# One queue instead of two for the opening loads of a sparse matmul

## The chip, the cores and the metric

The kernel runs on one core of one Trainium2 chip. The metric is the device time of one execution in microseconds; a time that is given for a kernel is the median of its runs. Beside the runs there is one profiled execution, from which every row of a view comes.

## The reference

Two of every four weights along the contraction axis are kept, those of largest magnitude, and the pruned matrix multiplies x; a bias is added.

```python
B, S, D = 16, 512, 1024            # x: (B, S, D), w: (D, D), b: (D), all bf16
wg = w.reshape(D // 4, 4, D)
mag = jnp.abs(wg)
order = jnp.argsort(mag, 1)
thr = jnp.take_along_axis(mag, order[:, 2:3, :], 1)     # the second largest of four
wp = (wg * (mag >= thr)).reshape(D, D)
return jnp.einsum("bsd,df->bsf", x, wp) + b
```

## The kernel before

x is taken as 8192 rows, in 64 tiles of 128 rows. TensorE (PE) does all products: for each tile, 8 slices of the contraction axis by 2 halves of 512 output columns, accumulated in PSUM. DVE adds the bias on the way out of PSUM and ACT's queue stores the tile.

The weights have to be pruned first. They are worked on in six pieces (`pieces`): four of 256 columns for the upper half of the contraction axis (group 0), then two of 512 columns for the lower half (group 1). For a piece, DVE takes magnitudes (`abs`), maxima and minima of pairs (`hi`, `lo`), the threshold (`t1`, `t2`, `thr`), a mask and the product of weight and mask (`mult`), which it writes to `wp`. For pieces 2 and 3 ACT takes the magnitudes. In `wp` the four members of a group of four lie beside each other in a partition, so x must be in the same order to be multiplied by it: that is done for x tiles 0 to 6, which are loaded in rows (`load_x`) and transposed on PE (`T3a` is the transpose of tile 3, four matmuls against an identity), copied out of PSUM by ACT (`C3a`), and multiplied by each piece as it becomes ready (`M3.0yp` is tile 3 with part of piece 0). The partial sums are staged in SBUF (`S`, `U`). Later tiles use `wp_nat`, the pruned weights in the natural order, to which SP's queue copies `wp` by DMA (`W0.0` and the like), and x that a transposing DMA on SP's queue has loaded (`xlead`, `xlow`, `xb`).

The order of instructions on PE, DVE, ACT and SP in the opening is written out by hand as four lists of such names, and `seq` ties each instruction to the one before it on its engine. Ahead of these lists stand the opening's loads, on SP's queue and on ACT's, and the fillers: PE multiplies a constant, first six times over 512 columns, then fourteen times over 128, before the first transpose. DVE's list begins with `abs0a abs0b hi0a lo0 hi0b`: the magnitudes of piece 0 in two halves. PE's begins with `T3a T4a T5a T6a T2a M3.0yp`, so tiles 3 and 4, then 5 and 6, then 2 are wanted in that order.

`LATE` is the number of last tiles whose result is stored in two halves, each as soon as it is ready, rather than in one.

The lines that the prediction names: L138 is the filler, L193 the transpose, L198 its copy by ACT, L169 and L159 DVE's pruning steps, L229 the products with `wp`, L242 those with `wp_nat`, L98 the call that issues a load, a spread or a store, L112 the transposing loads of `xlead`.

Of the kernel before, what the change touches and what calls it, by code (L numbers as in the profile page):

```python
# [11 lines left out]
def kernel(  # L12
# [30 lines left out]
    STG = 8  # L43
    SOLO = 6
    GROUPS = ((0, 3), (3, 6), (6, 7))
    LATE = 6
    sizes = (4, 8, 8, 8, 8, 8, 8)
    batches = []
    t0 = NPK + LEAD
# [23 lines left out]
    def pe(i):  # L73
        return seq("pe", i)
# [4 lines left out]
    def act(i):  # L79
        return seq("act", i)  # L80
# [15 lines left out]
    def issue(eng, out_, in_):  # L96
        q = nc.sync if eng == "sp" else nc.scalar
        return seq(eng, q.dma_start(out_, in_))  # L98

    def load_w(g, c0, c1, ma=0, mb=4, eng="sp"):  # L100
        issue(eng, w_sb[:, g, ma:mb, c0:c1], wv[:, g, ma:mb, c0:c1])

    def load_x(ta, tb, eng="sp"):
        xs = const.tile([P, tb - ta, HK], bf16, name=f"x_{ta}")
        issue(eng, xs[:], xf[ta * P:tb * P, :HK].rearrange("(t p) k -> p t k", p=P))
        for t in range(ta, tb):
            x_sb[t] = xs[:, t - ta, :]
# [7 lines left out]

    xnat, held = {}, {}

    load_w(0, 0, 256, 0, 2)
    load_w(0, 0, 256, 2, 4, "act")
    load_x(5, 7, "act")  # L120
    act(nc.scalar.activation(spark[:], nc.const_aps.tensor(1.0, [P, 1], bf16), Act.Abs))
    load_x(3, 5)
    load_x(2, 3)
    load_w(0, 256, 512)
    load_x(0, 2)
# [10 lines left out]
    def filler(n, rep=1):  # L136
        for _ in range(n):
            pe(nc.tensor.matmul(warm_ps[:, :rep * P], lhsT=nc.const_aps.tensor(1.0, [P, P], bf16),  # L138
                                rhs=nc.const_aps.tensor(1.0, [P, rep * P], bf16), start=True, stop=True))
# [251 lines left out]
    def run(queues):  # L391
        while any(queues.values()):
            moved = False
            for eng, toks in queues.items():
                while toks and all(n in written for n in needs(eng, toks[0])):
                    emit(eng, toks[0])
                    tok = toks.pop(0)
                    written.add(tok)
                    if tok[0] == "M" or tok[0].islower():
                        written.update(atoms(tok))  # L400
                    moved = True
            assert moved, queues

    filler(6, 4)
    filler(14)
    run({eng: order[eng].split() for eng in order})

    def load_nat(ta, tb):
# [26 lines left out]
    def evac(o, ps, c0, c1, add=None):  # L435
        if add is None:
            dve(nc.vector.tensor_tensor(o[:, c0:c1], ps, bias_sb[:, c0:c1], op=Alu.add))  # L437
        else:
            dve(nc.vector.tensor_tensor(o[:, c0:c1].rearrange("p (n c) -> p n c", n=2),  # L439
                                        ps.rearrange("p (n c) -> p n c", n=2), add, op=Alu.add))  # L440
# [4 lines left out]
    def store(eng, t, o, c0=0, c1=Dout):  # L445
        issue(eng, rows(t)[:, c0:c1], o[:, c0:c1])
# [25 lines left out]
    for bi, (tb, nb) in enumerate(batches):  # L472
        if bi:
            load_batch(bi + 1)
        for j in range(nb):
# [9 lines left out]
            else:  # L485
# [4 lines left out]
                for h in range(2):  # L490
                    evac(o, pss[h][:], h * FH, (h + 1) * FH)
                    if t >= NT - LATE:
                        store("act", t, o, h * FH, (h + 1) * FH)
                if t < NT - LATE:
                    store("act", t, o)
# [30 lines left out]
```

## Time and profile before

| what | us |
|---|---|
| median of 3 runs | 232.76 (232.62 to 232.9) |
| profiled execution | 232.89 |
| its span, first to last instruction | 231.1 |
| PE busy in the span | 226.6 |
| DVE busy | 107.9 |
| ACT busy | 14.0 |

The span is shorter than the execution's time by what lies around the first and last instruction. "Busy" for PE counts overlapping matmuls once, with modelled ends; the start-to-start distance of matmuls tells their pace. In a row of a timeline the first number is the start in us from the span's start, the second the duration of the group, then the engine (a q behind it is its queue or sequencer), the line, the operation, what is written and read, and how many instructions the row holds; in square brackets stands the idle time before it and what ended it. PEld is the load of a matmul's stationary operand. In a row of DMA issues the last number is the time from issue to landing.

### The profile page before, as it was taken

The page shows a single profiled execution, that of the slowest core. Times are in us where ns is not written, and L with a number is a line of the kernel's source. Part 1 is how long each engine was busy: PE and PEld are TensorE (multiplying, and loading weights), DVE is VectorE, ACT ScalarE, POOL GpSimd, SP SyncE. Part 2 cuts the span into 40 slices and gives each one's busy share as a digit, 9 for nine tenths or more (in the row PEclk, how much of TensorE's full clock was granted, in tenths as well). Part 3 has the DMA queues.
Part 4 walks back from the last instruction along what each step waited for, and adds up shares of the span by engine and source line. Part 5 has one row for each costly group of instructions (what it writes and reads, how often), then busy time and mean ns, then how long its engine had stood idle before and what let it go on. Part 6 is the DMA issues. An engine that isn't in the chain of part 4 may idle for free.

```text
span 231.1 us, 2851 instructions
## 1 busy us (share of the span) xinstructions
PE 226.6 (98%) x1142; PEld 110.9 (48%) x1162; DVE 107.9 (47%) x200; ACT 14.0 (6%) x27; POOL 17.6 (8%) x15
## 2 busy tenths in 40 slices
PE   8999999999999999999999999999999999999995
PEld 5986444444444444444444444444444444444443
DVE  3999877844424424424424424423423423433434
ACT  2874100000000000000000000000000000000000
POOL 1000199700000000000000000000000000000000
PEclk9999999999999999999999999999999999999999
DMA  6999999997399422991259821693128932122122
GB/s 203 276 197 280 164 217 223 297 320 252 124 206 232 155 91 72 237 281 64 75 116 252 222 94 71 162 298 134 65 91 198 273 122 83 54 91 91 53 86 91
DMA packets 79308, 38.19 MB, mean 165 GB/s; under 512 B 64192, under 2 KB 71744, under 8 KB 79296
## 3 DMA queue, kind: packets, MB, share of 16 engines
q1 hardware_dynamic: 68384, 20.75, 43.6%
q10 hardware_dynamic: 10912, 17.27, 20.9%
q8 instruction: 9, 0.15, 0.3%
q14 instruction: 3, 0.02, 0.0%
HBM read 3.28 MB, written 16.78 MB: 87 GB/s over the span
## 4 chain that ended last, share of the span: by engine, by line
PE 98%; issue 0%; DVE 0%
PE ps L242 88%; PE ps L229 5%; PE tp L242 2%; PE ps L138 2%; PE tp L193 1%; PE ps L193 0%; DVE o L437 0%
## 5 line engine op out<-in xcount | busy, mean ns | idle before, releaser
L242 PE MATMUL ps<-wp_nat,xb 128*128 128x512 bf16 (+1 forms) x831 | 178.9, 375 | 0.9
L242 PEld LDWEIGHTS <-xb 128*128 128x128 bf16 x848 | 82.2, 98 | 97.7
L437 DVE TENSOR_TENSOR o<-ps,bias_sb 128x512 bf16<-128x512 f32 (+1 forms) x112 | 71.6, 677 | 113.7 <-PE ps L242 111.4
L433 POOL TENSOR_TENSOR st<-st,bias_sb 128x1024 f32<-128x1024 f32 x8 | 16.7, 2142 | 0.0
L242 PE MATMUL ps<-wp_nat,xlead 128*128 128x512 bf16 x63 | 14.7, 379 | 0.1
L242 PEld LDWEIGHTS <-xlead 128*128 128x128 bf16 x88 | 8.6, 98 | 10.2
L229 PE MATMUL ps<-wp,xt 128*128 128x256 bf16 (+1 forms) x130 | 12.8, 258 | 0.0
L439 DVE TENSOR_TENSOR o<-ps,st 128x512 bf16<-128x512 f32 x16 | 11.1, 691 | 2.8 <-PE ps L242 2.2
L229 PEld LDWEIGHTS <-xt 128*128 128x128 bf16 x130 | 10.9, 98 | 1.1
L242 PE MATMUL ps<-wp_nat,xlow 128*128 128x512 bf16 x47 | 10.6, 379 | 0.1
L264 ACT COPY st<-ps 128x512 f32<-128x512 f32 x14 | 7.4, 600 | 3.2 <-PE ps L229 3.1
L242 PEld LDWEIGHTS <-xlow 128*128 128x128 bf16 x48 | 4.7, 98 | 5.7
L159 DVE TENSOR_TENSOR mag<-mag,hi 128x256 bf16<-128x256 bf16 (+2 forms) x15 | 6.1, 435 | 0.1
L159 DVE TENSOR_TENSOR wp<-w_sb,mag 128x256 bf16<-128x256 bf16 (+2 forms) x15 | 6.1, 435 | 0.1
L242 PE MATMUL tp<-wp_nat,xlead 128*128 128x512 bf16 x23 | 5.8, 380 | 0.0
L138 PE MATMUL ps<-const-bfloat16-1.0 128*128 128x128 bf16 (+1 forms) x20 | 4.2, 408 | 0.8 <-PEq L510 0.8
L169 DVE TENSOR_SCALAR mag<-w_sb 128x512 uint16<-128x512 uint16 (+2 forms) x5 | 2.3, 473 | 3.5 <-DMA w_sb<-in_w_dram 3.5
L138 PEld LDWEIGHTS <-const-bfloat16-1.0 128*128 128x128 bf16 x20 | 2.3, 146 | 2.4 <-issue 2.4
L159 DVE TENSOR_TENSOR hi<-mag 128x512 bf16<-128x512 bf16 (+2 forms) x7 | 3.2, 458 | 0.1
L159 DVE TENSOR_TENSOR lo<-mag 128x512 bf16<-128x512 bf16 (+1 forms) x6 | 3.1, 509 | 0.0
L193 PEld LDWEIGHTS <-x 128*128 128x128 bf16 x28 | 2.3, 124 | 0.3 <-DMA x<-in_x_dram 0.2
L422 POOL COPY pruned<-wp 128x1 bf16<-128x1 bf16 x1 | 0.2, 187 | 26.7 <-DVE wp L159 26.7
(18 smaller groups left out, 18.8 us busy)
## 6 DMA issues: line engine op xcount, KB each, us to landing
out_dram<-o ACTq DMA_DIRECT2D x58, 256.0 KB, 2.4
wp_nat<-wp SPq DMA_DIRECT2D x14, 128.0 KB, 3.2
out_dram<-o ACTq DMA_DIRECT2D x10, 128.0 KB, 1.7
w_sb<-in_w_dram SPq DMA_DIRECT2D x2, 512.0 KB, 5.5
w_sb<-in_w_dram SPq DMA_DIRECT2D x3, 256.0 KB, 5.1
x<-in_x_dram SPq DMA_DIRECT2D x2, 256.0 KB, 4.3
x<-in_x_dram ACTq DMA_DIRECT2D x1, 256.0 KB, 4.0
bias_sb<-in_b_dram SPq DMA_DIRECT2D x1, 256.0 KB, 4.7
```

Of the source, the lines that this page charges most:

```text
L138: pe(nc.tensor.matmul(warm_ps[:, :rep * P], lhsT=nc.const_aps.tensor(1.0, [P, P], bf16), rhs=nc.const_aps.tensor(1.0, [P, rep * P], bf16), ...
L159: dve(nc.vector.tensor_tensor(out, a, b_, op=op))
L169: dve(nc.vector.tensor_single_scalar(mag.bitcast(u16), w_.bitcast(u16), 0x7FFF, op=Alu.bitwise_and))
L193: pe(nc.tensor.transpose(tp[:, m, :], xg[:, m, :], ident[:]))
L229: pe(nc.tensor.matmul(ps[:, c0 + d:c1 + d], lhsT=xpk[t][:, m, :], rhs=wp[:, g, m, c0:c1], start=(new and m == ms.start), stop=(left[key] = ...
L242: pe(nc.tensor.matmul(ps, lhsT=xt[:, kt - koff, :], rhs=wp_nat[:, kt, c0:c1], start=(kt == first), stop=(kt == last)))
L264: act(nc.scalar.copy(staged[(q, h)][:, at, :, :].rearrange("p t c -> p (t c)"), ps_open.pop(key)[:]))
L422: pool(nc.gpsimd.tensor_copy(out=pruned[:], in_=wp[:, 1, 3, Dout - 1:]))
L433: pool(nc.gpsimd.tensor_tensor(st[:], st[:], bias.to_broadcast([P, 2, 2, CW]), op=Alu.add))
L437: dve(nc.vector.tensor_tensor(o[:, c0:c1], ps, bias_sb[:, c0:c1], op=Alu.add))
L439: dve(nc.vector.tensor_tensor(o[:, c0:c1].rearrange("p (n c) -> p n c", n=2), ps.rearrange("p (n c) -> p n c", n=2), add, op=Alu.add))
```

## The change

All loads of the opening go to SP's queue. The first weights (piece 0) come in one load of 256 KB instead of two of 128 KB on two queues. x tiles 5 and 6 move from ACT's queue to SP's, behind x tiles 3 and 4 and ahead of tile 2. ACT's table load (`spark`) thereby has no DMA issue ahead of it. Of the short fillers ten are left of fourteen. `LATE` goes from 6 to 7. DVE's list, with `abs0a` and `abs0b` apart, stays.

```diff
-    LATE = 6
+    LATE = 7
...
-    load_w(0, 0, 256, 0, 2)
-    load_w(0, 0, 256, 2, 4, "act")
-    load_x(5, 7, "act")
+    load_w(0, 0, 256)
+    load_x(3, 5)
     act(nc.scalar.activation(spark[:], nc.const_aps.tensor(1.0, [P, 1], bf16), Act.Abs))
-    load_x(3, 5)
+    load_x(5, 7)
     load_x(2, 3)
     load_w(0, 256, 512)
     load_x(0, 2)
...
     filler(6, 4)
-    filler(14)
+    filler(10)
```

## The prediction

> **What bounds the kernel now.** I read the page first: the share of each engine and the chain that ended last.
>
> ```profile
> PE 226.6 (98%) x1142; PEld 110.9 (48%) x1162; DVE 107.9 (47%) x200; ACT 14.0 (6%) x27; POOL 17.6 (8%) x15
> PE ps L242 88%; PE ps L229 5%; PE tp L242 2%; PE ps L138 2%; PE tp L193 1%; PE ps L193 0%; DVE o L437 0%
> ```
>
> TensorE is the chain from end to end, so a change at the start is worth what it moves TensorE's first useful work, if nothing later hands the time back. I then read the chain in order of time for the first 20 us, the counts of matmuls in two half-microseconds, and the waits of the first 16 us.
>
> ```profile
> 0.77 4.21 PE ps L138 x20
> 4.99 1.02 PE tp L193 x8
> 6.01 0.51 PE ps L193 x8
> 6.52 0.22 PE tp L193 x4
> ...
> 9.16 10.30 PE ps L229 x108
> ```
> ```profile
> 5.50:6.00 0.50, 0.50 (x7) 1.00 1.09 330
> 6.00:6.50 0.50, 0.50 (x12) 1.00 1.12 343
> ```
> ```profile
> DVE mag L169 <- DMA w_sb<-in_w_dram: 3.5, 1, 3.5
> PEld L193 <- DMA x<-in_x_dram: 0.2, 1, 0.2
> ```
>
> L138 is filler and L193 are the transposes of x. Three things are to be seen. Eight transposes take 1.02 us before 6.0 us and 0.51 us after it: TensorE runs at half pace until about 6.0 us and at full pace from there, although the granted clock (1.00, the number ahead of the DMA share) reads full in both. TensorE's one wait for data is 0.2 us, for the x tiles 3 and 4. And the DVE starts at 3.5 us, when the first weights land.
>
> **The fillers and the first transpose.**
>
> ```profile
> 3.29 1.43 PEld L138 LDWEIGHTS <-const-bfloat16-1.0 128*128 128x128 bf16 x13 [0.28 <-issue]
> 4.67 0.31 PE L138 MATMUL ps<-const-bfloat16-1.0 128*128 128x128 bf16 x1
> 4.96 0.30 PE L193 MATMUL tp<-ident,x 128*128 128x128 bf16 x1
> ```
>
> The six long fillers end where the short ones begin, near 3.29. The fourteenth short one starts at 4.67, so a short one takes (4.67 - 3.29) / 13 = 0.106 us. With ten they end at 3.29 + 10 x 0.106 = 4.35 instead of 4.78. Nothing else is queued between them and the first transpose, so that transpose can start at 4.35 at the earliest, against 4.96: 0.61 us sooner, if x has landed. But this time lies in the half-pace stretch. If that stretch still ends at 6.0 us, a transpose that fits before it saves only the 0.055 us (0.22 / 4) that it would have taken after it. The gain of an earlier start is therefore half: at most 0.61 / 2 = 0.31 us.
>
> **When x 3-4 land.**
>
> ```profile
> 0.73 0.45 SPq L98 DMA_DIRECT2D w_sb<-in_w_dram  x1
> 0.74 0.50 ACTq L98 DMA_DIRECT2D w_sb<-in_w_dram  x1
> 1.24 0.96 SPq L98 DMA_DIRECT2D x<-in_x_dram  x2
> 1.26 0.49 ACTq L98 DMA_DIRECT2D x<-in_x_dram  x1
> 2.25 0.68 SPq L98 DMA_DIRECT2D w_sb<-in_w_dram  x1
> ```
> ```profile
> w_sb<-in_w_dram SPq DMA_DIRECT2D x1, 128.0 KB, 2.7
> w_sb<-in_w_dram ACTq DMA_DIRECT2D x1, 128.0 KB, 2.9
> x<-in_x_dram SPq DMA_DIRECT2D x1, 256.0 KB, 3.7
> x<-in_x_dram ACTq DMA_DIRECT2D x1, 256.0 KB, 4.0
> 3.50:4.00 0.50, 0.50 (x7) 0.50 (x6) 0.50 (x3) 0.00 (x0) 0.00 (x0) 1.00 1.09 389
> ```
>
> Now x 3-4 (SP) and x 5-6 (ACT) are issued 0.02 us apart, share the DMA engines, and land at 1.24 + 3.7 = 4.94 and 1.26 + 4.0 = 5.26. After the change x 5-6 stand behind x 3-4. By 4.94 all of x 5-6 but the last 0.32 us' worth has moved, at 389 GB/s some 125 of its 256 KB; the other 131 KB no longer go ahead of x 3-4, which is 0.34 us: 4.60. If all 256 KB were out of the way it would be 0.66 us: 4.28. Against that, the whole first weight load takes 0.68 us to issue (the 256 KB row at 2.25) instead of 0.45, so x 3-4 are issued 0.23 us later, which costs nothing while the engines still move weights and 0.23 us if they don't: 5.17 at worst. I take 4.5, between the two bandwidth values, because the engines are saturated (share 1.09) and issue leads transfer by over a microsecond. The first transpose then starts at 4.52 and the gain is (4.96 - 4.52) / 2 = 0.22 us, with 0.31 and -0.10 as ends. The bytes ahead of x 5-6 and x 2 are the same as now, so they land no later than 5.26 and about as now; the tile 5 transposes start at 4.52 + 8 x 0.106 = 5.37, after that.
>
> **When the first weights land: what is late next.**
>
> ```profile
> 3.50 0.49 DVE L169 TENSOR_SCALAR mag<-w_sb 128x512 uint16<-128x512 uint16 x2 [3.50 <-DMA w_sb<-in_w_dram]
> 5.80 0.28 DVE L159 TENSOR_TENSOR wp<-w_sb,mag 128x256 bf16<-128x256 bf16 x1
> 6.58 0.22 PE L229 MATMUL ps<-wp,xt 128*128 128x128 bf16 x1
> ```
>
> The DVE's steps of piece 0 follow each other without a pause, so all of them move with the landing of the first load. The first product with pruned weights needs the 5.80 step, which ends at 6.08; TensorE comes for it at 6.58, so the margin is 0.50 us. One load of 256 KB instead of two halves makes the first abs step wait for all of it. Low bound: the first half's 0.73 + 2.7, about 3.45. High bound: a 256 KB load of the same time, 4.0 on ACT: 0.73 + 4.0 = 4.73. I take 3.65, the second half's landing (0.74 + 2.9 = 3.64): the same bytes on the same engines. [...] Then the DVE is 0.15 us late, the 5.80 step ends at 6.23, and TensorE, 0.22 us early, comes at 6.36: 0.13 us of margin remain. The ACT copies of the transposed tiles follow the transposes and move with them.
>
> **The other moves.** Each later load of SP is issued 0.23 + 0.46 (half of the 0.96 for two) = 0.69 us later.
>
> ```profile
> 2.96 0.61 SPq L98 DMA_DIRECT2D x<-in_x_dram  x1
> x<-in_x_dram SPq DMA_DIRECT2D x1, 256.0 KB, 5.0
> 8.33 0.39 PE L193 MATMUL tp<-ident,x 128*128 128x128 bf16 x4
> 12.49 0.28 DVE L159 TENSOR_TENSOR wp<-w_sb,mag 128x256 bf16<-128x256 bf16 x1
> 13.18 0.49 PE L229 MATMUL ps<-wp,xt 128*128 128x256 bf16 x3
> 11.53 3.50 SPq L98 DMA_DIRECT2D wp_nat<-wp  x4
> wp_nat<-wp SPq DMA_DIRECT2D x14, 128.0 KB, 3.2
> 19.30 1.03 PE L242 MATMUL tp<-wp_nat,xlead 128*128 128x512 bf16 x4
> out_dram<-o ACTq DMA_DIRECT2D x10, 128.0 KB, 1.7
> ```
>
> x 0-1 land at 2.96 + 5.0 = 7.96, and the queue holds enough work that 0.69 us of later issue doesn't show; tile 0 is transposed at 8.33 now, 8.11 then: margin 0.15. The products of column piece 2 start at 13.18 on weights ready at 12.77: margin 0.41, of which 0.22 goes and up to 0.15 more if the DVE is still late: 0.04. The spread of the first pruned half, on SP behind the loads and a transposing load, is at 11.53 for 3.50 and the last part lands 3.2 after its issue, near 17.4; 0.69 later that is 18.1, before its use at 19.3 - 0.22. Were that cover gone, its delay would go to TensorE one for one. The ACT table load moves up to 0.74 us and has nothing waiting behind it. LATE = 7 splits the store of one more tile, the seventh from the end; at 16 products of some 0.22 us a tile that is over 20 us before the end, against 1.7 us to land: nothing. Without that cover it would be one issue more, half a microsecond.
>
> **The sum.** -0.22 us from the opening, nothing else. The profiled execution has 231.1 us of span and took 232.89; it becomes 232.67. The median of the runs is 232.76, 0.13 lower, so the forecast is 232.54. From no change a measurement of this kernel can tell some 0.2%, which is 0.47 us. The forecast lies inside that.
>
> **Rivals.** (1) Slower: the half pace lasts longer. [...] For it: the fillers end 0.43 us sooner. Against it: the change of pace came 1.0 us into the transposes, so those did not stop it. [...] (2) Slower: the first weights land late because one queue alone starts slowly. The first product comes at landing + 2.63 (6.08 - 3.45), so it is even with now at 3.95, over 0.2% slower from 4.42, and at the high bound of 4.73 it is 7.36 against 6.58: +0.78, 233.5. For it: the two queues' halves now move at once. Against it: the engines, not the queues, are full from 3.5 us. (3) No gain: x 3-4 land near 4.94 as now: 0.0, 232.8; it needs the issue delay to show in full. (4) Faster than forecast: if the pace is released by unbroken work, the 0.18 us gap before 4.96 delays it now, and a full queue brings it sooner. Then TensorE is bound by the DVE: 6.58 - 6.11 = 0.47 with weights at 3.45, 232.3; the 0.41 margin of piece 2 caps it near there.
>
> **Chances.** Forecast 0.45 (0.06 of it beyond 0.2% faster, since runs of one kernel lie 0.28 us apart). Rival 1: 0.17, slower. Rival 2: 0.18, of which 0.11 slower, 0.07 within. Rival 3: 0.06, within. Rival 4: 0.14, of which 0.10 faster, 0.04 within. Together faster 0.16, within 0.2% 0.56, slower 0.28. The range runs from rival 4 less half the runs' spread (232.15) to rival 2 near its high bound (233.4) and leaves out rival 1. The likeliest case alone is 232.4 to 232.7.
>
> **What would show it.** Right: the wait of PEld L193 for x stays at 0.3 us or less with the first transpose at 4.3 to 4.6; the DVE's first step at 3.6 to 3.75; the pace doubles near 6.0; first product near 6.35; the group at 9.16 some 0.2 earlier. Wrong: a wait of PE L229 on DVE wp near 6.4 (rival 2), eight transposes still taking 1 us after 6.1 (rival 1), a wait of tile 0's transposes for x, or a first transpose near 4.95.

## The result, and the profile after

The change made the kernel slower. Its median is 233.34 us (14 runs, 232.79 to 235.11); the kernel before, run beside it, has 232.53 (14 runs, 232.33 to 233.0). The ratio is 1.0037, with a 95% interval of 1.0023 to 1.0051: about 0.86 us, beyond the 0.2% that a measurement of this kernel can tell. Three of the six runs of one kernel below (the late spread on ACT's queue, with x 5-6 on SP) were in a slower state, which its ratio leaves out and its median doesn't. The profiled execution of the changed kernel took 233.67 us with a span of 231.9; before it was 232.89 and 231.1, so it shows 0.8 us of the loss. Lines of the changed kernel are one lower than before: L137 is the filler, L192 the transpose, L228 the products with `wp`, L241 those with `wp_nat`, L168 the magnitudes.

The page of the changed kernel, its busy times and the lines of its chain:

```profile
PE 227.0 (98%) x1158; PEld 109.8 (47%) x1158; DVE 107.9 (47%) x200; ACT 14.0 (6%) x27; POOL 17.6 (8%) x15
PE ps L241 88%; PE ps L228 5%; DMA x<-in_x_dram 2%; PE tp L241 2%; SPq L98 1%; PE tp L192 0%; DVE o L436 0%; PE ps L192 0%
```

Busy times are as before. The chain is not: a DMA of x now has 2% of it, where before it was the fillers and the first transposes. The chain in order of time says which DMA (start, duration, what):

```profile
3.75 5.25 DMA x<-in_x_dram
9.00 0.05 issue
9.04 0.42 PE tp L192 x4
```

It is the load of x tiles 0 and 1, the last of SP's x loads: issued at 3.75, landed at 9.00, and tile 0's transposes start 0.04 us later. Before they started at 8.33. TensorE's timeline of the opening (start, duration, in brackets the idle time and what ended it):

```profile
4.64 0.64 PE L192 MATMUL tp<-ident,x 128*128 128x128 bf16 x8 [0.30 <-DMA x<-in_x_dram]
5.93 0.64 PE L192 MATMUL ps<-ident,x 128*128 128x128 bf16 x8 [0.66 <-DMA x<-in_x_dram]
6.41 0.39 PE L192 MATMUL tp<-ident,x 128*128 128x128 bf16 x4
6.63 1.92 PE L228 MATMUL ps<-wp,xt 128*128 128x128 bf16 x20
9.04 0.42 PE L192 MATMUL tp<-ident,x 128*128 128x128 bf16 x4 [0.49 <-DMA x<-in_x_dram]
...
20.10 0.81 PE L241 MATMUL tp<-wp_nat,xlead 128*128 128x512 bf16 x3
```

Before, TensorE waited for x once, for 0.2 us. Now it waits three times: for tiles 3 and 4 ahead of 4.64, for 5 and 6 ahead of 5.93, for 0 and 1 ahead of 9.04. The first two cost almost nothing against the kernel before: the first product is at 6.63, before it was at 6.58. They do take the gain that was forecast. At tile 0 the lateness grows from 0.05 to 0.71 us (9.04 against 8.33), so the third wait costs 0.66. Another 0.09 comes in small steps until 14 us, and the first product with `wp_nat` comes at 20.10 against 19.30: 0.80 us late, which is the whole difference of the spans. From there on both kernels are alike: TensorE's last matmul ends 209.13 us later in both, and the span 2.65 us after that, so nothing after 20 us adds or gives back.

The DVE waits for weights a second time:

```profile
3.87 0.49 DVE L168 TENSOR_SCALAR mag<-w_sb 128x512 uint16<-128x512 uint16 x2 [3.87 <-DMA w_sb<-in_w_dram]
...
8.22 0.43 DVE L168 TENSOR_SCALAR mag<-w_sb 128x1024 uint16<-128x1024 uint16 x1 [0.77 <-DMA w_sb<-in_w_dram]
```

The magnitudes of piece 1 start at 8.22 after 0.77 us of idling; before, piece 1 landed at 2.25 + 4.5 = 6.80 and the DVE had no such wait. So two loads came late together, x tiles 0 and 1 and the weights of piece 1. SP's queue as it issues, and the time from issue to landing of each load in the same order, from the DMA view of each stretch of the changed kernel:

```profile
0.73 0.68 SPq L98 DMA_DIRECT2D w_sb<-in_w_dram  x1
1.47 1.62 SPq L98 DMA_DIRECT2D x<-in_x_dram  x3
3.13 0.57 SPq L98 DMA_DIRECT2D w_sb<-in_w_dram  x1
3.75 0.62 SPq L98 DMA_DIRECT2D x<-in_x_dram  x1
```
```profile
w_sb<-in_w_dram SPq DMA_DIRECT2D x1, 256.0 KB, 3.1
x<-in_x_dram SPq DMA_DIRECT2D x1, 256.0 KB, 3.1
x<-in_x_dram SPq DMA_DIRECT2D x1, 256.0 KB, 3.8
x<-in_x_dram SPq DMA_DIRECT2D x1, 128.0 KB, 3.7
w_sb<-in_w_dram SPq DMA_DIRECT2D x1, 256.0 KB, 5.1
x<-in_x_dram SPq DMA_DIRECT2D x1, 256.0 KB, 5.3
```

| load | before: issue, landing | after: issue, landing | later by |
|---|---|---|---|
| first weights | 0.73 and 0.74, 3.66 | 0.73, 3.84 | 0.18 |
| x 3-4 | 1.24, 4.92 | 1.47, 4.59 | -0.33 |
| x 5-6 | 1.26, 5.31 | 2.12, 5.89 | 0.58 |
| x 2 | 1.75, 5.70 | 2.62, 6.30 | 0.60 |
| weights of piece 1 | 2.25, 6.80 | 3.13, 8.20 | 1.40 |
| x 0-1 | 2.96, 7.96 | 3.75, 9.00 | 1.04 |

Everything behind x 3-4 is late. The issue of x 0-1 moved 0.79 us, its landing 1.04. The bytes moved from 2 to 7 us, from the DMA view of that stretch, first of the kernel before, then of the changed one:

```profile
DMA packets 2256, 1.55 MB, mean 310 GB/s; under 512 B 111, under 2 KB 2256, under 8 KB 2256
```
```profile
DMA packets 1919, 1.36 MB, mean 271 GB/s; under 512 B 84, under 2 KB 1919, under 8 KB 1919
```

The same loads in another arrangement moved 0.19 MB less in these 5 us, which at 310 GB/s is 0.6 us of transfer. Little of it is the start, though the first packet moved at 2.20 us where it had moved at 1.83: by 4 us the changed kernel is 0.03 MB behind (263 against 279 GB/s from 2 to 4 us). The rest is a lower rate from 4 to 7 us, 276 against 331 GB/s.

### The profile page after: what moved, and what is told of

Read it like the earlier page. It is cut to its first block, busy times and chain, and to the rows that moved or that the text cites. A ratio compares the mean times of both kernels' runs of the same rounds, so it can differ in the third digit from the quotient of the medians.

```text
span 231.9 us, 2864 instructions
## 1 busy us (share of the span) xinstructions
PE 227.0 (98%) x1158; PEld 109.8 (47%) x1158; DVE 107.9 (47%) x200; ACT 14.0 (6%) x27; POOL 17.6 (8%) x15
## 4 chain that ended last, share of the span: by engine, by line
PE 95%; DMA 2%; SPq 1%; issue 0%; DVE 0%
PE ps L241 88%; PE ps L228 5%; DMA x<-in_x_dram 2%; PE tp L241 2%; SPq L98 1%; PE tp L192 0%; DVE o L436 0%; PE ps L192 0%
## 5 line engine op out<-in xcount | busy, mean ns | idle before, releaser
L241 PE MATMUL ps<-wp_nat,xb 128*128 128x512 bf16 (+2 forms) x848 | 179.8, 375 | 0.0
L241 PEld LDWEIGHTS <-xb 128*128 128x128 bf16 x848 | 82.4, 98 | 97.5
L241 PE MATMUL ps<-wp_nat,xlead 128*128 128x512 bf16 x64 | 14.8, 379 | 0.0
L241 PEld LDWEIGHTS <-xlead 128*128 128x128 bf16 x88 | 8.6, 98 | 10.2
L228 PE MATMUL ps<-wp,xt 128*128 128x256 bf16 (+1 forms) x130 | 12.8, 258 | 0.0
L228 PEld LDWEIGHTS <-xt 128*128 128x128 bf16 x130 | 10.8, 98 | 1.4
L241 PE MATMUL ps<-wp_nat,xlow 128*128 128x512 bf16 x48 | 10.7, 379 | 0.0
L241 PEld LDWEIGHTS <-xlow 128*128 128x128 bf16 x48 | 4.7, 98 | 5.7
L241 PE MATMUL tp<-wp_nat,xlead 128*128 128x512 bf16 x24 | 6.0, 379 | 0.0
L168 DVE TENSOR_SCALAR mag<-w_sb 128x512 uint16<-128x512 uint16 (+2 forms) x5 | 2.3, 474 | 4.6 <-DMA w_sb<-in_w_dram 4.6
L137 PE MATMUL ps<-const-bfloat16-1.0 128*128 128x128 bf16 (+1 forms) x16 | 3.6, 408 | 0.8 <-PEq L509 0.8
L137 PEld LDWEIGHTS <-const-bfloat16-1.0 128*128 128x128 bf16 x16 | 1.8, 138 | 2.4 <-issue 2.4
L192 PEld LDWEIGHTS <-x 128*128 128x128 bf16 x28 | 1.8, 115 | 2.1 <-DMA x<-in_x_dram 2.1
```

Source lines behind the costliest of these rows:

```text
L168: dve(nc.vector.tensor_single_scalar(mag.bitcast(u16), w_.bitcast(u16), 0x7FFF, op=Alu.bitwise_and))
L192: pe(nc.tensor.transpose(tp[:, m, :], xg[:, m, :], ident[:]))
L228: pe(nc.tensor.matmul(ps[:, c0 + d:c1 + d], lhsT=xpk[t][:, m, :], rhs=wp[:, g, m, c0:c1], start=(new and m == ms.start), stop=(left[key] = ...
L241: pe(nc.tensor.matmul(ps, lhsT=xt[:, kt - koff, :], rhs=wp_nat[:, kt, c0:c1], start=(kt == first), stop=(kt == last)))
```

## The experiments

Each kernel is the kernel before or the changed one with an edit; its ratio is against the kernel before, run on the same chip, with a 95% interval. Four explanations were open: the fillers (rival 1), the first weights (rival 2, S in the expectations: one 256 KB load starts later), the later loads, and the spread of pruned weights near 28 us, half of which SP's queue issues long after them (D: a late queue). The expectations call their explanations theories and give each a letter.

**The fillers alone.**

```diff
-    filler(14)
+    filler(10)
```

> The kernel before with ten short fillers instead of fourteen, nothing else. Theory A (the loads of the one queue land later, and that is the loss): x 3-4 still land near 4.9 us, TensorE idles some 0.6 us ahead of the first transpose, the end does not move: 232.5 us, within 0.1. Theory B (the shorter filling delays the full pace of TensorE, or makes its time vary): 233.0 to 233.5 us. Theory C (chance stalls of single DMA packets make the loss): 232.5.

232.64 us against 232.68, ratio 0.9997 (0.9987 to 1.0008). Its chain in order of time:

```profile
1.24 3.60 DMA x<-in_x_dram
...
4.89 0.64 PE tp L193 x8
...
6.22 1.92 PE ps L229 x20
```

Fewer fillers neither cost nor gain. In this execution TensorE was at full pace from 3.5 us, and the first product came at 6.22, though TensorE idled for x before 4.89.

**The changed kernel with its fillers back.**

```diff
-    filler(10)
+    filler(14)
```

> The changed kernel with fourteen short fillers again. Theory A: nothing comes back, 233.2 to 233.4 us, since the loads are as in the changed kernel. Theory B: the loss goes, 232.5 to 232.7 us. Theory C: as the changed kernel, 233.3, with as wide a spread.

233.62 us, ratio 1.0039 (1.0022 to 1.0057): the loss stays whole. Its x 5-6 landed at 6.50, TensorE waited 1.24 us for them, and its first product came at 7.25. Together the two runs take the fillers out of the question.

**The first weights in one load, nothing else of the change.**

```diff
-    load_w(0, 0, 256, 0, 2)
-    load_w(0, 0, 256, 2, 4, "act")
+    load_w(0, 0, 256)
```

> The kernel before with the first weights in one load on SP's queue; x tiles 5 and 6 stay on ACT's queue, fourteen fillers. Theory A: the weights land 0.36 us later as in the changed kernel, the DVE steps move by that, the margin of 0.50 us at the first product covers it and the later margins of 0.4 us just so: 232.5 to 232.7 us. Theory B and C: 232.5.

233.49 us, ratio 1.0041 (1.0021 to 1.0061). The DMA view of the opening, and a row of TensorE's timeline:

```profile
w_sb<-in_w_dram SPq DMA_DIRECT2D x1, 256.0 KB, 3.6
x<-in_x_dram ACTq DMA_DIRECT2D x1, 256.0 KB, 2.7
```
```profile
7.04 1.15 PE L228 MATMUL ps<-wp,xt 128*128 128x128 bf16 x13 [0.44 <-DVE wp L158]
```

The weights landed at 4.38, with x 5-6 at 3.45 ahead of them: ACT's load, issued at the same time, takes 0.46 us to issue instead of 0.68 and its packets went first: 203 of the 205 that moved until 2.7 us. TensorE then waited for the DVE and the first product came at 7.04, 2.66 after the weights. None of the three theories expected this loss. It is rival 2 as the prediction wrote it (landing + 2.63), but it needs ACT's load in front. In the changed kernel nothing is in front and the weights landed at 3.84.

**x 5-6 on SP's queue, nothing else of the change.**

```diff
-    load_x(5, 7, "act")
     act(nc.scalar.activation(spark[:], ...))
     load_x(3, 5)
+    load_x(5, 7)
```

> The kernel before with x tiles 5 and 6 on SP's queue behind tiles 3 and 4; the first weights stay in halves on two queues, fourteen fillers. Theory A: tiles 5-6 land near 5.6 us instead of 5.3 and the second weight piece and tiles 0-1 0.3 to 1.0 us later, so TensorE waits for tile 0: 232.8 to 233.3 us. Theory B: 232.5. Theory C (any load may have a stalled packet, more so the later ones): 232.5 in the median with single runs up to 235.

233.58 us, ratio 1.0035 (1.0019 to 1.0052): this edit alone costs as much as the whole change. In this execution the opening was in time (first product 6.32, first `wp_nat` product 19.04), but a row of TensorE's timeline shows a wait further on:

```profile
29.05 1.24 PE L242 MATMUL ps<-wp_nat,xlead 128*128 128x512 bf16 x5 [1.00 <-DMA wp_nat<-wp]
```

A spread of pruned weights, issued at 23.99, landed at 29.01; in the kernel before the same one was issued at 22.98 and took 3.53 us instead of 5.02. That is theory D's place, not theory A's, though the time is above what A gave. Several of the edits below tried D.

**x 5-6 of the changed kernel back on ACT's queue, behind the table load.**

```diff
     load_w(0, 0, 256)
     load_x(3, 5)
     act(nc.scalar.activation(spark[:], ...))
-    load_x(5, 7)
+    load_x(5, 7, "act")
```

> The changed kernel with x tiles 5 and 6 on ACT's queue, issued behind ACT's table load at about 2.2 us, so that they cannot get ahead of the first weights; SP's queue is one load shorter. Theory A1 (the loss is the lateness of what stands behind x 5-6 on SP's queue: x 5-6 themselves, tile 2, the second weight piece, tiles 0-1): most of it comes back, 232.6 to 232.9 us; the first weights land near 3.85 and leave the first product its margin. Theory A2 (the loss is the first weights' own lateness): 233.2 to 233.4. Theory D (the loss is the spread of the pruned weights late in the opening, near 29 us): partly back, 232.8 to 233.1.

233.68 us, ratio 1.0066 (1.0047 to 1.0085). The edit did not do what it was for, as ACT's timeline shows:

```profile
0.74 1.28 ACT L120 ACT_TABLE_LOAD   x1 [0.74 <-PEq L509]
0.80 0.44 ACTq L98 DMA_DIRECT2D x<-in_x_dram  x1
```

The issue did not wait for the table load ahead of it. So x 5-6 went ahead of the weights again (3.63 and 4.48) and the first product was at 7.14, 2.66 after the weights. x 0-1 were in time, at 7.30: with one load fewer on SP, the loss at tile 0 is gone and rival 2's is there. All three theories gave less time than was measured.

**The kernel before with x 5-6 behind the table load.**

```diff
-    load_x(5, 7, "act")
     act(nc.scalar.activation(spark[:], ...))
+    load_x(5, 7, "act")
```

> The kernel before with x tiles 5 and 6 still on ACT's queue but issued behind ACT's table load, about 1.3 us later; all else, the first weights in halves included, as before. Theory A1: x 5-6 land near 5.6 us instead of 5.3, the first product comes 0.1 to 0.4 us later in executions where TensorE has its full pace early and not later in the others: 232.6 to 232.9. Theories A2 and D: 232.6, as before.

232.47 us, ratio 0.9999 (0.999 to 1.0008). For the same reason the load was issued at 1.32 instead of 1.26, so this tells no more than a repeat of the kernel before. Its full pace began at 3.8 us and its first product came at 6.16.

**The late spread on ACT's queue instead of SP's,** in the kernel with x 5-6 on SP and in the changed one.

```diff
-            "S2b3 U7h0 W1.0q U7h1"
+            "S2b3 U7h0 W1.0 U7h1"
...
-            "W0.0 Z W0.1 X1 W1.0p X2 Y1 Y0 W1.1"
+            "W0.0 Z W0.1 X1 X2 Y1 Y0 W1.1"
```

> The kernel before with x tiles 5 and 6 on SP's queue (233.58 us), and the spread of the third half of the pruned weights (four copies that close to 29 us are waited for) wholly on ACT's queue instead of half on SP's. Theory D (SP's queue, 0.7 us late, brings this spread too late and TensorE waits 1.2 us at 29 us): the loss goes, 232.5 to 232.8. Theory A1: the spread is not what costs in most executions, 233.3 to 233.6.

> The changed kernel with the same spread wholly on ACT's queue. Theory D: 232.6 to 232.9. Theory A1: no change, 233.3, since the loss lies before 10 us.

237.58 us (six runs, 234.83 to 239.21), ratio 1.0138 (1.0112 to 1.0165), and 235.48, ratio 1.0124 (1.0094 to 1.0154). Both got worse, and neither expectation was met. On ACT the four parts are issued one behind the other and the last lands at 30.68 in the first kernel and 31.58 in the second, so the edit made a later spread of its own. One of the waits from 25 to 35 us in the second kernel, and the window of TensorE from 32 to 34 us in the first (the stretch, its length, PE's busy time and matmuls, the granted clock, the DMA share, GB/s):

```profile
PE ps L241 <- DMA wp_nat<-wp: 1.5, 1, 1.5
```
```profile
32.00:34.00 2.00, 2.00 (x6) 0.50 1.04 199
```

They don't decide on D. They do show that TensorE waits for a late spread, and that in the first kernel half pace came on top of the wait.

**SP's queue later, without touching x 5-6.** Two loads of 512 bytes behind the last opening load.

```diff
+    for n in range(2):
+        more = const.tile([P, 2], bf16, name=f"more{n}")
+        issue("sp", more[:], b[256 * n:256 * n + 256].rearrange("(p k) -> p k", p=P))
```

> The kernel before with two more loads of 512 bytes each on SP's queue, behind the last weight load of the opening and ahead of the first transposing load; nothing of the opening's loads moves, but the queue is some 1.0 us later from there on. Theory D (the queue's lateness reaches the spread of the pruned weights that is waited for near 28 us): a wait there of up to 1.2 us, 232.8 to 233.6. Theory A1 (only the landings before 10 us cost): 232.5, within 0.15.

232.65 us, ratio 1.001 (1.0001 to 1.0018): about 0.2 us (0.02 to 0.42 by the interval). There is no wait near 28 us, but the edit didn't make the spreads late. SP's queue, at the first transposing load and the first spread:

```profile
6.70 4.62 SPq L112 DMA_TRANSPOSE xlead<-in_x_dram  x1
11.44 3.34 SPq L98 DMA_DIRECT2D wp_nat<-wp  x4
```

The transposing load is 1.13 us later than in the kernel before (5.57), but it took 4.62 us to issue instead of 5.84, and the first spread is issued at 11.44 as against 11.53. With x 5-6 on SP's queue it is at 12.54, in the changed kernel at 12.44. So this run doesn't test theory D. What speaks against D for the changed kernel is its own trace: TensorE had no wait after 20 us. For the kernel with x 5-6 on SP and nothing else, D stays open.

**One load less on SP in the kernel with x 5-6 there:** the bias is loaded by ACT's queue, later.

```diff
-            "C3a C4a C5a C6a C2a S0b0 C0a C1a abs2 S3b0 S2b0 abs3 S0b1 U6h0 S3b1 S2b1 S0b2 S3b2 S2b2 S0b3 U6h1 S3b3 "
+            "C3a C4a C5a C6a C2a S0b0 C0a C1a abs2 S3b0 S2b0 abs3 S0b1 B U6h0 S3b1 S2b1 S0b2 S3b2 S2b2 S0b3 U6h1 S3b3 "
...
-            sp(nc.sync.dma_start(bias_sb[:], b.partition_broadcast(P)))
+        elif tok[0] == "B":
+            act(nc.scalar.dma_start(bias_sb[:], b.partition_broadcast(P)))
```

> The kernel before with x tiles 5 and 6 on SP's queue (233.58 us), and the load of the bias taken from SP's queue to ACT's, behind the sixth of its copies, which gives SP's queue back the 0.65 us that the x load cost it. Theory D: the spread near 28 us comes in time again, 232.5 to 232.8. Theory A1: 233.3 to 233.6.

232.89 us, ratio 1.0019 (1.0005 to 1.0032), where the kernel with x 5-6 on SP had 1.0035. No wait near 28 us is left; this execution waited for x 0-1, which landed at 8.76. About half of the loss went, which neither theory gave, and the two intervals overlap. So moving x 5-6 makes several loads late, and which of them TensorE feels differs from one execution to the next.

**The first weights of the changed kernel in halves, both on SP.**

```diff
-    load_w(0, 0, 256)
+    load_w(0, 0, 256, 0, 2)
+    load_w(0, 0, 256, 2, 4)
```

> The changed kernel with the first weights in two halves again, both on SP's queue. Theory S (a load's first packet starts a fixed time behind the end of its issue, so the longer issue of one whole load delays all that follows): the first packet is at 1.83 us instead of 2.2, the first half lands near 3.3, the second near 3.65, x 5-6 near 5.5, and TensorE's first product comes near 6.3; what is left of the loss is then what the queue's lateness costs further on: 232.8 to 233.3 us. Theory T (the single queue itself is slow, whatever the size of its first load): x 5-6 land at 5.9 or later, 233.3 to 233.8.

233.53 us, ratio 1.004 (1.0026 to 1.0054). Two rows of TensorE's timeline:

```profile
6.34 1.92 PE L229 MATMUL ps<-wp,xt 128*128 128x128 bf16 x20
8.95 0.41 PE L193 MATMUL tp<-ident,x 128*128 128x128 bf16 x4 [0.69 <-DMA x<-in_x_dram]
```

Theory S holds for the start: the first packet moved at 1.83 again, the halves landed at 2.96 and 3.51, and the first product came at 6.34, 0.24 sooner than in the kernel before. All of it was lost at tile 0, for which x landed at 8.91. The start is not the loss; the loads behind it are.

**Fewer loads.** x 3 to 6 as one load, in the changed kernel:

```diff
-    load_x(3, 5)
-    load_x(5, 7)
+    load_x(3, 7)
```

> The changed kernel with x tiles 3 to 6 in one load of 512 KB instead of two of 256 KB: one issue fewer on SP's queue, all four tiles land together. Theory A1: they land near 5.2 to 5.4, the transposes then run through at full or half pace, tile 2, the second weight piece and tiles 0-1 come 0.3 to 0.5 us earlier than in the changed kernel: 232.8 to 233.1. Theory T: no better, 233.3.

Seven of twelve runs took 232.99 to 233.09 us and five 234.82 to 235.18; the ratio over all is 1.0055 (1.0031 to 1.0079). The profiled one took 234.93. In it no load behind the first weights was held up (piece 1 landed at 6.72, x 0-1 at 7.51), but x 3-6 landed at 5.49, and TensorE idled 0.98 us before it. Its windows (the stretch, its length, PE's busy time and matmuls, the granted clock, the DMA share, GB/s):

```profile
6.00:7.00 1.00, 1.00 (x12) 1.00 1.10 319
9.00:10.00 1.00, 1.00 (x8) 1.00 1.09 345
10.50:11.50 1.00, 1.00 (x15) 1.00 1.16 260
```

Half pace lasted until 10.3 us. Theory P: that stretch of idle time keeps TensorE at half pace, and makes the five long runs. It was tried with more fillers ahead of it (the next expectation puts the idle time at 1.3 us, which is that of the weight loads; TensorE's matmuls paused for 0.98):

```diff
-    filler(10)
+    filler(22)
```

> The changed kernel with x tiles 3 to 6 in one load (12 runs: seven near 233.0 us, five at 234.8 to 235.2) and twenty-two short fillers instead of ten, so that TensorE has no idle time of 1.3 us ahead of the first transpose. Theory P (the runs two microseconds longer are those where this idle time keeps TensorE at half pace): no run near 235 is left, all within 232.8 to 233.3. Theory Q (they come from late loads): such runs remain.

233.29 us, ratio 1.0022 (1.0013 to 1.0032), all twelve runs between 232.92 and 233.6. The same windows:

```profile
6.00:7.00 1.00, 1.00 (x20) 1.00 1.06 252
9.00:10.00 1.00, 1.00 (x15) 1.00 1.10 369
```

None of twelve runs is long where five of twelve were, and 20 and 15 matmuls stand where 12 and 8 stood. So the fillers took away the long runs, which cost about 1.9 us each (234.8 to 235.2 against 233.0), and the one that was profiled is long by half pace, not by late loads. That idle time keeps the half pace, as theory P says, isn't shown: with 22 fillers TensorE still idled 1.06 us ahead of its first transpose, but it had been at full pace from 3.5 us. And x 0-1 landed at 8.34, so that with eight loads on SP most of the changed kernel's loss is still there.

The same single load of x 3 to 6 in the kernel before, with the weight halves still on two queues and fourteen fillers:

```diff
-    load_x(5, 7, "act")
...
-    load_x(3, 5)
+    load_x(3, 7)
```

> The kernel before with x tiles 3 to 6 in one load of 512 KB on SP's queue; the first weights in halves on two queues, fourteen fillers. Theory L (what slows the loads is x 5-6 as a load of its own behind x 3-4 on one queue): the bytes moved by 7 us stay at those of the kernel before, x 3-6 land near 5.0 us, the first product comes at 6.1 to 6.6: 232.5 to 232.8 us. Theory T (one queue for x is slow in any form): 233.2 to 233.6.

232.82 us, ratio 1.0008 (0.9996 to 1.002): no loss that can be told from none, with all of x on SP. x 3-6 landed at 5.05 and x 0-1 at 7.12. The bytes from 2 to 7 us:

```profile
DMA packets 2302, 1.59 MB, mean 318 GB/s; under 512 B 96, under 2 KB 2302, under 8 KB 2302
```

So it isn't the move of x to SP's queue as such. x 5-6 cost when they stand there as a load of their own, the ninth load on SP where there are eight here as before. Theory N takes the number of loads to be the reason.

**More loads.** The changed kernel with x 5 and x 6 apart, ten loads on SP:

```diff
-    load_x(5, 7)
+    load_x(5, 6)
+    load_x(6, 7)
```

> The changed kernel with x tile 5 and x tile 6 in a load each on SP's queue, one load more, the same bytes. Theory N (it is the number of loads on one queue that slows them): x 5 and 6 land later than in the changed kernel, fewer bytes are moved by 7 us than its 1.3 MB, 233.6 to 234.2 us. Theory L (it is this pair of loads as they are cut now): as the changed kernel or better, 232.9 to 233.4.

233.8 us, ratio 1.0054 (1.0035 to 1.0073). x 6 landed at 6.50 and x 0-1 at 8.97; the bytes from 2 to 7 us:

```profile
DMA packets 1844, 1.27 MB, mean 254 GB/s; under 512 B 95, under 2 KB 1844, under 8 KB 1844
```

The bytes went the way that N says; the time went that way too, but its interval overlaps the changed kernel's. Over all profiled executions, by the number of opening loads that each queue holds (the two small loads, which stand behind all others, aren't counted):

| loads on SP | on ACT | kernels | MB from 2 to 7 us | x 0-1 landed |
|---|---|---|---|---|
| 8 | 2 | before; ten fillers; x 5-6 behind the table load; two small loads added | 1.55 to 1.61 | 7.10 to 7.96 |
| 8 | 1 | first weights in one load; changed with x 5-6 on ACT; before with x 3-6 in one | 1.56 to 1.59 | 7.12 to 8.08 |
| 8 | 0 | changed with x 3-6 in one, 10 and 22 fillers | 1.55, 1.40 | 7.51, 8.34 |
| 9 | 1 | x 5-6 on SP; the same with the late spread, or the bias, on ACT | 1.38 to 1.49 | 7.44 to 8.76 |
| 9 | 0 | changed; with 14 fillers; with the late spread on ACT | 1.26 to 1.36 | 8.71 to 9.00 |
| 10 | 0 | changed with halves; changed with x 5 and 6 apart | 1.39, 1.27 | 8.91, 8.97 |

With a ninth load on SP no execution moved more than 1.49 MB; of the nine with eight, eight moved 1.55 or more. The waits go with it. In all eight executions with x 5-6 in loads of their own on SP's queue, TensorE waited for x 5-6 or for x 0-1, for 0.29 to 1.25 us; of the other nine none has such a wait of over 0.15 us, but for the two of the changed kernel with x 3 to 6 in one load, which wait for that load.

The packet records show where the time goes: a load landed when the slowest of its 16 DMA engines was done, and single packets of 512 bytes or 1 KB stalled. In the changed kernel fifteen engines had x 0-1 at 7.90, in time for tile 0, and the sixteenth at 9.00; for piece 1 it was 7.05 and 8.20. One packet took 1.94 us, from 5.17 to 7.11, which fits an engine that is behind at both, but the record doesn't name its engine. It isn't always one engine: with 14 fillers fifteen engines had x 0-1 only at 8.70, and the last at 8.71. From 2.5 to 9 us the kernels with x 5-6 as a load of its own on SP's queue have 14 to 42 packets of over 100 ns, those without 6 to 14, and the two with x 3 to 6 in one load behind one weight load 25 and 26. Why the packets stall, and whether the number of loads is the reason or only goes with it, stays open: those two kernels have many stalls with eight loads, and each profile is one draw. No kernel here beats the kernel before.

## Why the prediction was wrong

The forecast was 232.54 us with 0.56 for no difference that can be told; the measured 233.34 lies in the range of 232.15 to 233.4, but it is slower, which had 0.28. That it lies in the range is luck: the upper end came from rival 2, which is not what happened.

**The step that failed** is the end of the part on x 3-4 and the first of the other moves: "The bytes ahead of x 5-6 and x 2 are the same as now, so they land no later than 5.26 and about as now", and for x 0-1 "the queue holds enough work that 0.69 us of later issue doesn't show". Both take it that the engines stay as full whatever the arrangement of loads. They did not: 1.36 MB moved from 2 to 7 us where 1.55 had. x 5-6 landed at 5.89, x 2 at 6.30, and x 0-1 at 9.00 where 8.11 was needed. The text gave x 0-1 a margin of 0.15 us and used the queue's depth as its cover; it did not price that cover's loss. Without that cover x 0-1 land at 7.96 + 0.69 = 8.65, which is 0.32 later than tile 0's old start of 8.33 and a rival on the slower side; none of the four was this one, though a wait of tile 0 for x stands among the signs of being wrong. Of the 0.71 us by which tile 0 was late, 0.32 is this, 0.10 that the issue moved 0.79 and not 0.69, 0.25 that the load took 5.25 us instead of 5.0, and 0.04 the start after the landing. Against the forecast of -0.22 us the whole comes to 1.02: the first product 0.27 later than the 6.36 that was worked out, for x 5-6, then 0.66 at tile 0 and 0.09 in small steps.

**One queue or two.** For the first weights the text took the landing of the halves, "the same bytes on the same engines". There it held within 0.18 us (3.84 against 3.66). For the queue as a whole the arrangements differ by more than the issue: in one execution of each kernel, the issue of x 0-1 moved 0.79 us and its landing 1.04, piece 1 by 0.88 and 1.40. ACT's queue as such wasn't needed for x: in the kernel before, x 3 to 6 in one load on SP cost nothing measurable (1.0008).

**Fillers and x 3-4.** Right: 4.59 for the landing, 4.64 for the first transpose, against 4.5 and 4.52. But the half pace that the gain was worked out from ended at 4.0 us in this execution, not near 6.0. The windows of the changed kernel:

```profile
3.50:4.00 0.50, 0.50 (x7) 1.00 1.09 371
4.00:4.50 0.50, 0.34 (x6) 1.00 0.92 313
...
6.00:6.50 0.50, 0.50 (x10) 1.00 1.09 248
```

Seven matmuls before 4.0, then six in two thirds of a window. In the kernels with the kernel before's opening loads it ended at 3.5, 3.8, 5.9 and 6.0 us. The 6.0 was a draw of one execution. Where full pace came early, an earlier transpose only waited longer for x 5-6 (0.66 us here), and the 0.22 us gain was not there.

**The first weights.** Predicted 3.65, measured 3.84: the packets started after the load's issue, which was 0.23 us longer, and 0.37 us later than before; the prediction had the DVE 0.15 us late. The margin of 0.13 would not have held: the step of the DVE that the first product needs ended at 6.44, 0.08 after the 6.36 at which TensorE was to come. It wasn't felt, since the first product was at 6.63 for lack of x 5-6. Rival 2's formula was right where its condition came true, at 7.04 and 7.14 for weights at 4.38 and 4.48. It is not what happened here.

**Rival 1** is not what made the median: ten fillers alone changed nothing, and fourteen gave nothing back. Half pace ended during the transposes in several executions (at 5.2 us with the weight halves on SP, at 6.2 in the kernel before with x 3 to 6 in one), so transposes did not stop it there. No run shows what ends the half pace, nor whether transposes in place of fillers make it last, since fillers ran before them: the 0.17 was the author's estimate. That a longer half pace costs some 1.9 us is shown by the long runs of one kernel, of which one was profiled (half pace until 10.3 us). A longer half pace may be behind the changed kernel's single run of 235.11, but of that run there is no trace.

**Rival 4**'s 6.11 for the first product doesn't follow from the text's own landing + 2.63, which gives 6.08; it changes nothing here. That unbroken work releases the pace was its author's assumption, and no run shows it.

**The rest held.** `LATE` and everything after 20 us cost nothing: 209.13 us in both to the last matmul, and 2.65 behind it. The spread of the first half landed at 18.03, where 18.1 was forecast, and was in time.

## What to carry to other kernels

When loads are moved to one queue, work out each later load's landing with its delay of issue showing in full, and set that against the margin of its user; a queue that looks deep is not a cover until a row shows it. Look at the loads on the queue as well as at their bytes: in the kernel before, one load of x 3 to 6 on SP cost nothing that can be told (1.0008), where two cost 0.8 us. In the changed kernel the single load left most of the loss, so try it there rather than count on it. And take the point where TensorE reaches full pace (3.5 to 6.0 us in the kernels that open like the kernel before) from several executions before you price a gain by it.

## What the runs showed of the hardware

- In the kernel before and the changed one the first packet moved 0.65 and 0.79 us after the end of the first load's issue: at 1.83 us for a load that is issued in 0.45 us from 0.73, at 2.20 for one of 0.68.
- Of two loads of 256 KB issued together on two queues, the packets of the one with the shorter issue went first: 0.46 us against 0.68 with the first weights in one load, where the other's began at 2.69 us. In the changed kernel with x 5-6 on ACT's queue the shorter issue took 0.44 us, and the other's packets began at 2.91.
- A DMA issue on ACT's queue didn't wait for the table load ahead of it: it was issued at 0.80, the table load ran from 0.74 to 2.02; in the other kernel with this order it was issued at 1.32, the table load ran from 1.25 to 2.53.
- A load was as late as its last DMA engine: x 0-1 of the changed kernel were there at 7.90 on fifteen of sixteen and at 9.00 on the last, and their first transpose started at 9.04.
- Half pace at the start didn't show in the granted clock. With x 3 to 6 in one load it read 1.00 in the windows with 12 and 8 matmuls in a microsecond, as it did with 22 fillers in those with 20 and 15; at 32 us, after a wait, it read 0.50 in the kernel with x 5-6 on SP and the late spread on ACT's queue (6 matmuls in 2 us).
